# Two decode-attention problems in one kernel: batches of both taken in turn, weights in rings, loads in an order that a plan works out

## Chip, core and metric

The kernel runs on one core of one Trainium2 chip. The metric is device time in microseconds. Before the change the median of 6 runs is 285.73 us (282.39 to 287.11).

## What is computed

Two problems, A and B, each one token of grouped-query attention with 32 query heads on 16 key/value heads of 128, and a cache of 8,192 keys per head. A looks at the last 2,048 keys, B at all 8,192. All data are bfloat16. The result is the two output rows of 576, side by side.

```python
q = (x @ wq).reshape(B, Sq, Hq, Dh).transpose(0, 2, 1, 3)        # x: 1x1x576, wq: 576x4096
k = jnp.repeat(k_cache[:, :, Sk - W:, :], rep, axis=1)           # A: W = 2048; B: all 8192
v = jnp.repeat(v_cache[:, :, Sk - W:, :], rep, axis=1)           # rep = 2
scores = jnp.einsum("bhqd,bhkd->bhqk", q, k) * (Dh ** -0.5)
o = jnp.einsum("bhqk,bhkd->bhqd", softmax(scores), v)
out = o.transpose(0, 2, 1, 3).reshape(B, Sq, Hq * Dh) @ wo       # wo: 4096x576
```

Every byte is read once: per head 2.1 MB of keys and as much of values for B, 0.52 MB each for A, and per problem 4.7 MB of `wq` and of `wo`; in sum 102.8 MB.

## The kernel before

**Tiles and groups.** A key/value head of B has T = 64 tiles of 128 keys, one of A has 16. TensorE works in *groups* of eight tiles (GS = 8): 8 groups per head of B, 2 per head of A, 160 in all. For each group TensorE transposes eight key tiles into PSUM (`pe_tg`, L434), VectorE copies them to SBUF (`dve_copy`, L552), and TensorE multiplies them with the two query rows of the head (`pe_sg`, L458), one group behind.

**Batches.** Heads are put into batches; B has four of 4 heads, A has 4, 4, 4, 2 and 2 (`bsizes`). All of B comes first, then all of A. At the end of a batch its scores get a maximum (`dve_d1` L563, `pe_mxt` L470, `dve_d2d3` L572/L575, `pe_mxb` L477), ScalarE takes the exponentials (`act_batch` L599/L608), TensorE multiplies with the values (*PV*, `pe_pv` L487), sums the exponentials (`pe_z` L500), VectorE divides (`dve_norm` L584/L587), and TensorE multiplies with `wo` (`pe_outproj` L527), a 512-wide and a 64-wide matmul per query head. The whole problem is summed in one PSUM row (`bankP`), which ScalarE copies out at the end of each problem (`act_outcopy` L622/L625). The query projections (`pe_qproj_block` L410) are done in 16 blocks of four query heads.

**Order on TensorE.** It is fixed when the program is built. `hook` hangs a task behind the score step of a group, and never behind the last group, `NG - 1`. With L a batch's last group: `mxt` behind L+1, `mxb` behind L+3, the PVs of its heads behind L+6 and then every `dv` groups (8 for B, 2 for A), never before the PV of an earlier batch (`last_pv_pos`), the sum of exponentials with the last PV, the output projection four groups later. Tasks of one position keep the order in which they were hung. Query block number jg is hung behind group 5 jg - 1 or just before the first group of its heads, whichever is earlier.

**Loads.** All loads go through SyncE's queue, which issues in order and waits, where it must, for the buffer to be free; what is queued behind a waiting load waits too. Keys (L355) and values (L366) have three buffers each of one B head (2.1 MB), which also take four A heads each; `assign_regions` hands out places round and round, keys in the order of the heads, values in the order of the PVs. A key load waits for the last transposes, a value load for the PV, of the heads that had the place before. `wq` has two buffers (L320 and L325, a wait on the projection two blocks back), `wo` has a place for everything (L339). The loads are sorted by the place in TensorE's order at which they are needed:

```python
for h in heads:
    add_load(tindex[("tg", head_first_group[h["n"]])], (lambda h=h: dma_k(h, KQ)))
for h in heads:
    add_load(tindex[("pv", h["n"])] - 0.3, (lambda h=h: dma_v(h, KQ)))
loads.sort(key=lambda t: (t[0], t[1]))
for _, _, fn in loads:
    fn()
```

Of the kernel before, what the change touches and what calls it, by code (L numbers as in the profile page):

```python
# [125 lines left out]
def bass_concat_heads__sliding_block_cached__gqa_block_cached__decode_kernel(  # L126
# [14 lines left out]
    Dh = 128  # L141
# [15 lines left out]
    for pi, (x, kc, vc, wq, wo, nkeys, s0, ooff) in enumerate(  # L157
        [
            (B_x, B_k_cache, B_v_cache, B_wq, B_wo, Sk, 0, NOUT),
            (A_x, A_k_cache, A_v_cache, A_wq, A_wo, W, Sk - W, 0),  # L160
        ]
    ):
        T = nkeys // 128
        GS = min(8, T)
        assert T % GS == 0
        BH = min(Hkv, 512 // (rep * T), 4)
        G_ = T // GS
        bmin = max(1, -(-3 // G_))
        if pi == 1 and Hkv >= BH + 2 * max(2, bmin):
            tsz = max(2, bmin)  # L170
            bsizes = []
            left = Hkv - 2 * tsz
            while left > 0:
                bsizes.append(min(BH, left))
                left -= min(BH, left)
            bsizes += [tsz, tsz]
        else:
            bsizes = []
            left = Hkv
            while left > 0:  # L180
                bsizes.append(min(BH, left))
                left -= min(BH, left)
        assert sum(bsizes) == Hkv and all(0 < b <= BH for b in bsizes)
        probs.append(
            dict(pi=pi, x=x, k=kc, v=vc, wq=wq, wo=wo, T=T, s0=s0, GS=GS,
                 G=T // GS, BH=BH, bsizes=bsizes, NB=len(bsizes), ooff=ooff)
        )
# [5 lines left out]
    NS = 2  # L193

    with ExitStack() as es:
# [4 lines left out]
        wq_sb = [sb(f"wq_sb{i}", [128, NCH, HBQ * Dh], BF16) for i in range(2)]  # L200
        wo_sb = [sb(f"wo_sb{i}", [128, Hq, NOUT], BF16) for i in range(2)]
# [14 lines left out]
        outrow_sb = [sb(f"outrow{i}", [1, NOUT], BF16) for i in range(2)]  # L216

# [20 lines left out]
        for j in range(2):  # L238
            sems[f"wq{j}"] = sem(f"s_wqslot{j}")
        S = _Sched()  # L240

        heads = []
        for p in probs:
            bstart = []
            acc = 0
            for bsz in p["bsizes"]:
                bstart.append(acc)
                acc += bsz
            for g in range(Hkv):
                b = max(i for i in range(len(bstart)) if bstart[i] <= g)  # L250
                heads.append(dict(pi=p["pi"], g=g, T=p["T"], GS=p["GS"], G=p["G"],
                                  b=b, gl=g - bstart[b], qb=(g * rep) // HBQ))
# [15 lines left out]
        for p in probs:  # L268
            for b in range(p["NB"]):
                hs = [h for h in heads if h["pi"] == p["pi"] and h["b"] == b]  # L270
                batches.append(dict(pi=p["pi"], b=b, heads=hs,
                                    last_group=head_last_group[hs[-1]["n"]],
                                    first_group=head_first_group[hs[0]["n"]]))
# [32 lines left out]

        def wq_slot(pi, j):
            return (pi * NQB + j) % 2

        def dma_wq_block(p, j, q):  # L310
            pi = p["pi"]
            wq = p["wq"]
            c0, c1 = j * HBQ * Dh, (j + 1) * HBQ * Dh
            jg = pi * NQB + j
            slot = jg % 2
            waits = []
            if jg - 2 >= 0:
                pj = jg - 2
                waits.append(("pe", "qproj", pj // NQB, pj % NQB))
            S.add(q, lambda e: e.dma_start(wq_sb[slot][:, 0:nfull, :],  # L320
                                           wq[0:nfull * 128, c0:c1].rearrange("(c p) n -> p c n", p=128)),
                  waits=waits, inc=("wqdma", pi, j, 0), sem=f"wq{slot}")
            if D % 128:
                r = D % 128
                S.add(q, lambda e: e.dma_start(wq_sb[slot][0:r, nfull, :], wq[nfull * 128:D, c0:c1]),  # L325
                      inc=("wqdma", pi, j, 1), sem=f"wq{slot}")
# [3 lines left out]

        def dma_wo_batch(bt, q):
            pi = bt["pi"]
            p = probs[pi]
            hq0 = bt["heads"][0]["g"] * rep
            hq1 = (bt["heads"][-1]["g"] + 1) * rep
            semname = f"wo{bt['gb']}"
            if semname not in sems:
                sems[semname] = sem("s_" + semname)
            S.add(q, lambda e: e.dma_start(wo_sb[pi][:, hq0:hq1, :],  # L339
                                           p["wo"][hq0 * 128:hq1 * 128, :].rearrange("(h p) n -> p h n", p=128)),  # L340
                  inc=("wodma", bt["gb"]), sem=semname)
# [28 lines left out]

        def dma_out(p, q):
            pi, ooff = p["pi"], p["ooff"]
            S.add(q, lambda e: e.dma_start(out[0, 0:1, ooff:ooff + NOUT], outrow_sb[pi][0:1, :]),
                  waits=[("act", "oc2", pi)], inc=("outdma", pi), sem="out")
# [44 lines left out]
        def pe_tg(gi):  # L419
# [8 lines left out]
            if gi - NS >= 0:  # L428
                waits.append(("dve", "copy", gi - NS))
# [9 lines left out]
        def pe_sg(gi):  # L439
# [7 lines left out]
            waits = [("dve", "copy", gi)]  # L447
# [65 lines left out]
        def pe_outproj(bt):  # L513
            pi, gb = bt["pi"], bt["gb"]
            p = probs[pi]
            waits = [("dve", "oT", gb), ("wodma", gb)]
            if bt["b"] == 0 and pi == 1:
                waits.append(("act", "oc2", 0))
# [4 lines left out]
            lastbatch = (bt["b"] == p["NB"] - 1)  # L523
            for hq in range(hq0, hq1):
                for (c0, w) in out_chunks:
# [4 lines left out]
                        rhs=wo_sb[pi][:, hq, c0:c0 + w],  # L530
                        start=(hq == 0), stop=(hq == Hq - 1))),
                        waits=waits if k == 0 else [],
                        inc=(("pe", "outproj", pi) if lastbatch else ("pe", "outprojb", gb)) if last else None,
# [8 lines left out]

        def dve_copy(gi):
# [4 lines left out]
            bank = gi % NS  # L548
            waits = [("pe", "tg", gi)]
            if gi - NKT >= 0:  # L550
                waits.append(("pe", "sg", gi - NKT))
            S.add("dve", lambda e: e.tensor_copy(KTsb[kt][:, 0:GS, :], stage[bank][:, 0:GS * 128].rearrange(  # L552
                "p (g d) -> p g d", g=GS)),
                waits=waits, inc=("dve", "copy", gi), pb={"r": [f"S{bank}"]})
# [64 lines left out]
        def act_outcopy(p):  # L619
            pi = p["pi"]  # L620
            n1 = min(512, NOUT)
            S.add("act", lambda e: e.activation(outrow_sb[pi][0:1, 0:n1], bankP[0:1, 0:n1], ACT.Copy),  # L622
                  waits=[("pe", "outproj", pi)], inc=("act", "oc1", pi), pb={"r": ["P0"]})
            if NOUT > n1:
                S.add("act", lambda e: e.activation(outrow_sb[pi][0:1, n1:NOUT], bankP[0:1, n1:NOUT], ACT.Copy),  # L625
                      waits=[("act", "oc1", pi)], inc=("act", "oc2", pi), pb={"r": ["P1"]})
            else:
                S.add("act", lambda e: e.activation(outrow_sb[pi][0:1, 0:1], bankP[0:1, 0:1], ACT.Copy),
                      waits=[("act", "oc1", pi)], inc=("act", "oc2", pi), pb={"r": ["P0"]})
# [13 lines left out]
        for bt in batches:  # L643
            L = bt["last_group"]
            p = probs[bt["pi"]]
            dv = p["G"]
            pm = hook(L + 1, ("mxt", bt))
# [49 lines left out]

        TUNIT = min(p["T"] for p in probs)
# [36 lines left out]
        LEADW = 300  # L735
# [11 lines left out]
        wloads = []  # L747
        _lseq = [0]

        def add_load(pos, fn, lst=None):  # L750
            _lseq[0] += 1
            (loads if lst is None else lst).append((pos, _lseq[0], fn))

        for h in heads:
            add_load(tindex[("tg", head_first_group[h["n"]])], (lambda h=h: dma_k(h, KQ)))
        for p in probs:
            pi = p["pi"]
            add_load(min(tindex[("xt", pi)], tindex[("qproj", pi, 0)]) - 0.7, (lambda p=p: dma_x(p, WQ)),
                     wloads)
            for j in range(NQB):  # L760
                add_load(tindex[("qproj", pi, j)] - 0.5, (lambda p=p, j=j: dma_wq_block(p, j, WQ)), wloads)
        for h in heads:
            add_load(tindex[("pv", h["n"])] - 0.3, (lambda h=h: dma_v(h, KQ)))
        for bt in batches:
            add_load(tindex[("outprojb", bt["gb"])] - 0.2, (lambda bt=bt: dma_wo_batch(bt, KQ)))
        if WQ == KQ:
            loads = loads + wloads
            wloads = []
        loads.sort(key=lambda t: (t[0], t[1]))
        for _, _, fn in loads:  # L770
            fn()
        wloads.sort(key=lambda t: (t[0], t[1]))
        for _, _, fn in wloads:
            fn()
# [4 lines left out]
        cust = {"Q": [], "O": []}  # L779
        for kind, arg in pe_tasks:  # L780
# [37 lines left out]
            elif kind == "outprojb":  # L818
                bt = arg
                p = probs[bt["pi"]]  # L820
                pe_outproj(bt)
                if bt["b"] == p["NB"] - 1:
                    act_outcopy(p)
# [59 lines left out]
```

## Time and profile before

| | |
|---|---|
| device time, 6 runs | 285.22, 286.31, 285.30, 286.16, 282.39, 287.11 us; median 285.73 |
| the profiled execution | 284.68 us, of it 282.8 us span (first to last instruction) |
| busy share of the span | TensorE 84%, its weight loads 75%, VectorE 43%, ScalarE 8% |
| mean granted TensorE clock | 0.725 of full speed |
| DMA | 103.38 MB, mean 366 GB/s; SyncE's queue 94.5% and instruction fetch 0.8% of the 16 DMA engines' span |
| median from issue to landing | keys of B 14.7 us, values of B 15.8, `wo` of B 12.1, first part of `wq` of B 6.4 |

Columns of the groups below: line, engine, operation, output and input, count | busy us, mean ns of one | idle time of the engine before them and what ended most of it.

```profile
L552 DVE COPY ktsb<-stage 128x1024 bf16<-128x1024 bf16 x160 | 109.6, 691 | 103.9 <-PE stage L434 103.3
L434 PE MATMUL stage<-ident_b,kbuf 128*128 128x128 bf16 x1280 | 135.7, 270 | 18.9 <-issue 11.2
...
L458 PE MATMUL sc<-qT,ktsb 128*128 128x2 bf16 x1280 | 60.5, 168 | 11.0 <-issue 4.7
...
L487 PE MATMUL bankO<-pT,vbuf 128*128 128x2 bf16 x1280 | 36.8, 164 | 5.6 <-issue 3.7
```

TensorE carries the key transposes, the scores and the PVs; matmuls are pipelined, so the mean time of one is longer than its share of the busy time. "stage", "sc", "bankO", "bankP" and "bankQ" are PSUM tiles, "kbuf" and "vbuf" the buffers of keys and values. VectorE's idle time is mostly a wait for transposes. In the profile SyncE's queue is "SPq", and DMA share can pass 1 a little, because packets of one engine overlap.

### The profile page before, as it was taken

Reading aid. Unit: us, or ns where it says so; the run is one execution under the profiler, and the core shown is the slowest. Engines: PE = TensorE matmul, PEld = TensorE weight load, DVE = VectorE, ACT = ScalarE, POOL = GpSimd, SP = SyncE. Lnnn points to the kernel's source line nnn. Section 1 sums busy time; section 2 is a strip of 40 time slices with the busy share of each in tenths; the row PEclk is TensorE's granted clock in tenths of the full one; section 3 lists DMA queues with packets and bytes.
Section 4 is the critical chain, followed back from the end, with each engine's and each line's share of the span. In section 5 each row is a group of like instructions: output and inputs, shape, how many; then the busy total and the mean of one; then the engine's idle time right before and its main releaser. Section 6 shows DMA issues by size and latency. Waiting matters only on the chain.

```text
span 282.8 us, 9590 instructions
## 1 busy us (share of the span) xinstructions
PE 237.7 (84%) x4343; PEld 212.0 (75%) x4343; DVE 122.6 (43%) x225; ACT 23.1 (8%) x142; POOL 1.3 (0%) x9
## 2 busy tenths in 40 slices
PE   1699988999596999999968999589698899778775
PEld 1598887899596985998968798579577898774442
DVE  0257664545253551453534556346245466511010
ACT  1000000300000000300000030000002303302002
POOL 1000000000000000000000000000000000000000
PEclk9999995556657655955757588676877579955985
DMA  7989999999999999999999999999999975589990
GB/s 262 364 295 348 387 354 384 400 361 403 378 378 396 382 414 383 386 431 420 420 404 423 421 426 422 413 376 412 417 388 411 405 316 199 208 281 396 405 348 6
DMA packets 31935, 103.38 MB, mean 366 GB/s; under 512 B 2196, under 2 KB 19608, under 8 KB 27800
## 3 DMA queue, kind: packets, MB, share of 16 engines
q1 hardware_dynamic: 31896, 102.77, 94.5%
q8 instruction: 35, 0.57, 0.8%
q14 instruction: 4, 0.03, 0.0%
HBM read 102.76 MB, written 0.00 MB: 363 GB/s over the span
## 4 chain that ended last, share of the span: by engine, by line
PE 72%; DVE 10%; issue 9%; DMA 6%; ACT 1%; SPq 1%; DVEq 0%
PE stage L434 35%; PE bankO L487 11%; PE sc L458 10%; DVE ktsb L552 8%; PE bankQ L410 7%; PE bankP L527 6%; DMA wo_sb<-in_A_wo_dram 3%; DMA kbuf<-in_B_k_cache_dram 3%; PE bankQ L477 1%; PE bankO L500 1%; DVE mx L563 1%; SPq L366 1%; ACT pT L608 1%; PE bankQ L470 1%; DVE rz L584 0%
## 5 line engine op out<-in xcount | busy, mean ns | idle before, releaser
L552 DVE COPY ktsb<-stage 128x1024 bf16<-128x1024 bf16 x160 | 109.6, 691 | 103.9 <-PE stage L434 103.3
L434 PE MATMUL stage<-ident_b,kbuf 128*128 128x128 bf16 x1280 | 135.7, 270 | 18.9 <-issue 11.2
L434 PEld LDWEIGHTS stage<-ident_b,kbuf 128*128 128x128 bf16 x1280 | 102.7, 122 | 21.6 <-issue 13.1
L458 PE MATMUL sc<-qT,ktsb 128*128 128x2 bf16 x1280 | 60.5, 168 | 11.0 <-issue 4.7
L458 PEld LDWEIGHTS sc<-qT,ktsb 128*128 128x128 bf16 x1280 | 55.5, 106 | 16.6 <-DVE ktsb L552 9.4
L487 PE MATMUL bankO<-pT,vbuf 128*128 128x2 bf16 x1280 | 36.8, 164 | 5.6 <-issue 3.7
L487 PEld LDWEIGHTS bankO<-pT,vbuf 128*128 128x128 bf16 x1280 | 35.0, 99 | 6.8 <-issue 6.7
L527 PE MATMUL bankP<-wo_sb,oT 128*1 128x512 bf16 (+1 forms) x128 | 23.1, 346 | 3.9 <-DMA wo_sb<-in_A_wo_dram 2.4
L599 ACT ACTIVATE bias<-bankQ 128x8 f32<-128x8 f32 (+1 forms) x9 | 1.6, 177 | 250.4 <-PE bankQ L477 250.4
L410 PE MATMUL bankQ<-xT,wq_sb 128*128 128x1 bf16 (+1 forms) x320 | 20.2, 170 | 2.2 <-DVE xT L396 1.0
L410 PEld LDWEIGHTS bankQ<-xT,wq_sb 128*128 128x128 bf16 (+1 forms) x320 | 17.4, 100 | 4.5 <-DVE xT L396 1.2
L527 PEld LDWEIGHTS bankP<-wo_sb,oT 128*1 128x1 bf16 x128 | 8.6, 96 | 16.0 <-issue 10.4
L608 ACT ACTIVATE pT<-sc,bias 128x64 bf16<-128x64 f32 (+1 forms) x64 | 18.0, 316 | 0.3
L584 DVE RECIPROCAL rz<-bankO 128x8 f32<-128x8 f32 (+1 forms) x9 | 1.8, 202 | 30.8 <-PE bankO L500 30.8
L608 ACT ACTIVATION_READ_ACCUMULATOR pT<-sc,bias 128x1 f32 x64 | 13.7, 214 | 0.0
L540 DVE CAST qT<-bankQ 128x4 bf16<-128x4 f32 x16 | 2.6, 162 | 15.2 <-PE bankQ L410 15.2
L477 PE MATMUL bankQ<-diag,ones_f 8*128 8x8 f32 (+1 forms) x18 | 4.3, 308 | 0.6 <-DVE diag L575 0.6
L500 PE MATMUL bankO<-rsum,ones_f 128*128 128x8 f32 (+1 forms) x18 | 4.5, 325 | 0.0
L572 DVE TENSOR_REDUCE m<-bankQ 8x1 f32<-8x128 f32 (+1 forms) x9 | 2.4, 271 | 4.8 <-PE bankQ L470 4.8
L477 PEld LDWEIGHTS bankQ<-diag,ones_f 8*128 8x128 f32 (+1 forms) x18 | 3.5, 238 | 1.0 <-DVE diag L575 0.9
L563 DVE TENSOR_REDUCE mx<-sc 128x8 f32<-128x512 f32 (+2 forms) x9 | 4.0, 446 | 0.5 <-PE sc L458 0.5
L500 PEld LDWEIGHTS bankO<-rsum,ones_f 128*128 128x128 f32 x18 | 3.9, 270 | 0.0
(20 smaller groups left out, 13.8 us busy)
## 6 DMA issues: line engine op xcount, KB each, us to landing
vbuf<-in_B_v_cache_dram SPq DMA_DIRECT2D x16, 2048.0 KB, 15.8
kbuf<-in_B_k_cache_dram SPq DMA_DIRECT2D x16, 1792.0 KB, 14.7
kbuf<-in_A_k_cache_dram SPq DMA_DIRECT2D x32, 256.0 KB, 10.5
vbuf<-in_A_v_cache_dram SPq DMA_DIRECT2D x16, 512.0 KB, 7.9
wo_sb<-in_B_wo_dram SPq DMA_DIRECT2D x4, 1152.0 KB, 12.1
kbuf<-in_B_k_cache_dram SPq DMA_DIRECT2D x16, 256.0 KB, 10.7
wq_sb<-in_B_wq_dram SPq DMA_DIRECT2D x8, 512.0 KB, 6.4
wq_sb<-in_A_wq_dram SPq DMA_DIRECT2D x8, 512.0 KB, 8.5
```

The lines of the kernel that those rows point to most:

```text
L366: S.add(q, lambda e: e.dma_start(Vbuf[slot][:, row0:row0 + T, :], p["v"][0, g, s0:s0 + T * 128, :].rearrange("(p t) d -> p (t d)", p=128)) ...
L410: S.add("pe", (lambda e, hq=hq, c=c, rows=rows: e.matmul(bankQ[:, QT_COL[pi] + hq:QT_COL[pi] + hq + 1], lhsT=wq_sb[slot][0:rows, c, (hq - ...
L434: S.add("pe", (lambda e, i=i, t=t: e.transpose(stage[bank][:, i * 128:(i + 1) * 128], Kbuf[slot][:, krow + t, :], ident_b[:, :])), waits=w ...
L458: S.add("pe", (lambda e, i=i, col=col: e.matmul(sc[bank][:, col:col + rep], lhsT=KTsb[kt][:, i, :], rhs=qT_sb[pi][:, g * rep:(g + 1) * rep ...
L470: S.add("pe", lambda e: e.transpose(bankQ[0:nh, MXT_COL:MXT_COL + 128], mx_sb[pi][:, c0:c0 + nh], ident_f[:, :]), waits=[("dve", "d1", gb) ...
L477: S.add("pe", lambda e: e.matmul(bankQ[:, BIAS_COL:BIAS_COL + nh], lhsT=ones_f[0:nh, :], rhs=diag_sb[pi][0:nh, 0:nh], start=True, stop=Tru ...
L487: S.add("pe", (lambda e, t=t: e.matmul(bankO[:, col:col + rep], lhsT=Vbuf[slot][:, vrow + t, :], rhs=pT_sb[pi][:, g, t, :], start=(t == 0) ...
L500: S.add("pe", lambda e: e.matmul(bankO[:, Z_COL[pi] + c0:Z_COL[pi] + c0 + nh], lhsT=ones_f[:, :], rhs=rsum_sb[pi][:, c0:c0 + nh], start=Tr ...
L527: S.add("pe", (lambda e, hq=hq, c0=c0, w=w: e.matmul(bankP[0:1, c0:c0 + w], lhsT=oT_sb[pi][:, hq:hq + 1], rhs=wo_sb[pi][:, hq, c0:c0 + w], ...
L552: S.add("dve", lambda e: e.tensor_copy(KTsb[kt][:, 0:GS, :], stage[bank][:, 0:GS * 128].rearrange("p (g d) -> p g d", g=GS)), waits=waits, ...
L563: S.add("dve", lambda e: e.tensor_reduce(mx_sb[pi][:, c0:c0 + nh * rep], sc[bank][:, 0:nh * T * rep].rearrange("p (g t h) -> p g h t", g=n ...
L608: S.add("act", (lambda e, g=g, gl=gl, r=r, hq=hq, col0=col0: e.activation(pT_sb[pi][:, g, :, r], sc[bank][:, col0:col0 + T * rep].rearrang ...
```

## The change

- **Order of batches.** Batches of B and A are taken in turn, in proportion to their number. A's batches become 4, 4, 4, 3 and 1 heads.
- **Rings.** `wq` gets eight buffers for two. `wo` gets four buffers of one batch each, in place of one place for all heads; a load waits for the projection four batches back.
- **Accumulation.** Each batch's output projection is a sum of its own in `bankP`, and VectorE adds it to a row in SBUF (`dve_outacc`); ScalarE's copies at the end of a problem are gone. An output projection waits for the sum of the one before it.
- **Spacing.** The last batch of a problem, other than the very last batch, gets another `dv` for its PVs.
- **Order of loads.** Each load has a place where its buffer becomes free (`ready`), one where it is needed (`need`), and its bytes. When the program is built, a loop steps through TensorE's order with assumed durations and an assumed bandwidth, and issues, as long as fewer than 5 MB are on their way, the load with the earliest need among the ready ones. Only the order that comes out of it is used.
- `COPY_ACT_EVERY`, by which ScalarE could take a part of the key copies, is 0.

```diff
-        if pi == 1 and Hkv >= BH + 2 * max(2, bmin):
-            tsz = max(2, bmin)
+        if pi == 1 and Hkv >= BH + bmin + 2:
...
+            if bmin > 1:
+                tail = [bmin + 1, 1]
...
-            bsizes += [tsz, tsz]
+            bsizes += tail
...
+    NWQ = 8
+    NWO = 4
+    COPY_ACT_EVERY = 0
...
-        wq_sb = [sb(f"wq_sb{i}", [128, NCH, HBQ * Dh], BF16) for i in range(2)]
-        wo_sb = [sb(f"wo_sb{i}", [128, Hq, NOUT], BF16) for i in range(2)]
+        wq_sb = [sb(f"wq_sb{i}", [128, NCH, HBQ * Dh], BF16) for i in range(NWQ)]
+        BQMAX = max(max(p["bsizes"]) for p in probs) * rep
+        wo_sb = [sb(f"wo_sb{i}", [128, BQMAX, NOUT], BF16) for i in range(NWO)]
...
+        while ia < len(la) or ib < len(lb):
+            if ia < len(la) and (ib >= len(lb) or ia * len(lb) <= ib * len(la)):
+                order.append(la[ia])
+                ia += 1
+            else:
+                order.append(lb[ib])
+                ib += 1
         heads = []
...
+        for hs in order:
+            heads.extend(hs)
...
+            waits = []
+            if gb - NWO >= 0:
+                waits.append(ev_outproj_done(batches[gb - NWO]))
+            S.add(q, lambda e: e.dma_start(wo_sb[slot][:, 0:hq1 - hq0, :],
                                            p["wo"][hq0 * 128:hq1 * 128, :].rearrange("(h p) n -> p h n", p=128)),
...
-        def pe_outproj(bt):
+        def pe_outproj(bt, xw=()):
...
-            waits = [("dve", "oT", gb), ("wodma", gb)]
-            if bt["b"] == 0 and pi == 1:
-                waits.append(("act", "oc2", 0))
+            waits = [("dve", "oT", gb), ("wodma", gb)] + list(xw)
...
-                        rhs=wo_sb[pi][:, hq, c0:c0 + w],
-                        start=(hq == 0), stop=(hq == Hq - 1))),
+                        rhs=wo_sb[gb % NWO][:, hq - hq0, c0:c0 + w],
+                        start=(hq == hq0), stop=(hq == hq1 - 1))),
...
-        def act_outcopy(p):
...
+        def dve_outacc(bt):
...
+            if b == 0:
+                dst = outrow_sb[pi] if lastb else oacc_sb[pi][0]
+                S.add("dve", lambda e: e.tensor_copy(dst[0:1, :], bankP[0:1, 0:NOUT]),
+                      waits=[("pe", "outprojb", gb)], inc=("dve", "oacc", gb), pb={"r": banks})
             else:
+                src = oacc_sb[pi][(b - 1) % 2]
+                dst = outrow_sb[pi] if lastb else oacc_sb[pi][b % 2]
+                S.add("dve", lambda e: e.tensor_tensor(dst[0:1, :], bankP[0:1, 0:NOUT], src[0:1, :], ALU.add),
+                      waits=[("pe", "outprojb", gb), ("dve", "oacc", gb - 1)], inc=("dve", "oacc", gb),
+                      pb={"r": banks})
...
+            if bt["gb"] < len(batches) - 1 and bt["b"] == p["NB"] - 1:
+                dv = max(3, -(-p["T"] * 35 // (p["GS"] * 92)))
...
         for h in heads:
-            add_load(tindex[("tg", head_first_group[h["n"]])], (lambda h=h: dma_k(h, KQ)))
+            ready = max([tindex[("tg", head_last_group[m])] for m in h["kprev"]], default=-1)
+            T = h["T"]
+            add_load(ready, tindex[("tg", head_first_group[h["n"]])], (lambda h=h: dma_k(h, KQ)),
+                     T * 128 * 128 * 2, 2 if T > h["GS"] else 1, ("k", h["n"]))
...
+            ready = max([tindex[("pv", m)] for m in h["vprev"]], default=-1)
+            add_load(ready, tindex[("pv", h["n"])], (lambda h=h: dma_v(h, KQ)),
+                     h["T"] * 128 * 128 * 2, 1, ("v", h["n"]))
...
+        BW = 370e3
+        ISSUE_NS = 0.65
+        INFLIGHT = 5.0e6
...
+        for i in range(len(pe_tasks)):
+            kind, arg = pe_tasks[i]
+            while True:
+                now = t_pe
+                inflight_bytes[:] = [(tc, b) for (tc, b) in inflight_bytes if tc > now]
+                if sum(b for _, b in inflight_bytes) >= INFLIGHT:
+                    break
+                cands = [by_seq[q] for q in pending_set if by_seq[q]["ready"] < i]
+                if not cands:
+                    break
+                ld = min(cands, key=lambda d: (d["need"], d["seq"]))
+                issue(ld, now)
+            for ld in loads_of_task.get(i, []):
+                if ld["seq"] in pending_set:
+                    assert ld["ready"] < i
+                    issue(ld, t_pe)
...
+            t_end[i] = start + task_dur(kind, arg)
+            t_pe = t_end[i]
...
+        for ld in loads_in_order:
+            ld["fn"]()
...
-                pe_outproj(bt)
-                if bt["b"] == p["NB"] - 1:
-                    act_outcopy(p)
+                pe_outproj(bt, xw=cust["P"])
+                dve_outacc(bt)
+                cust["P"] = [("dve", "oacc", bt["gb"])]
```

## The prediction

> **What bounds the kernel now.** I read the table of stretches first, because shares over the whole span mix stages. Columns: us, busy time of each engine, granted TensorE clock, DMA share, GB/s.
>
> ```profile
> 14.00:28.00 14.00, 13.67 (x249) 12.81 (x247) 8.86 (x16) 0.00 (x0) 0.00 (x0) 1.00 0.89 319
> 28.00:42.00 14.00, 12.88 (x265) 11.51 (x262) 9.09 (x16) 0.00 (x0) 0.00 (x0) 0.99 1.04 368
> 42.00:224.00 182.00, 158.78 (x2905) 146.12 (x2901) 84.24 (x145) 11.50 (x75) 0.00 (x0) 0.65 1.03 402
> 224.00:252.00 28.00, 24.60 (x596) 23.30 (x593) 15.30 (x32) 6.14 (x46) 0.00 (x0) 0.80 0.69 256
> 252.00:273.00 21.00, 16.88 (x232) 10.51 (x230) 2.01 (x8) 2.11 (x11) 0.00 (x0) 0.80 1.05 394
> 273.00:282.80 9.80, 5.35 (x53) 2.96 (x51) 0.84 (x4) 2.11 (x11) 0.00 (x0) 0.55 0.21 76
> ```
>
> From 42 to 224 us the DMA never rests (1.03) while TensorE idles 23 of 182 us: problem B is bound by transfers. DMA rests only in four places. With 1.03 as full, they are worth 1.9 us in the first 7 us (share 0.75 there), 14 x (1 - 0.89/1.03) = 1.9 at 14 to 28, 28 x (1 - 0.69/1.03) = 9.2 at 224 to 252, and 9.8 x (1 - 0.21/1.03) = 7.8 at the end. Their sum is 20.8, so the queue share, 95.3% of 282.8 us, is 262 us of full DMA. I use this as a clock: x MB of the 102.8 have landed at 1.9 + 2.55x us at the earliest.
>
> Next SyncE's waits (us in total, times, longest), and its issues around the largest hole (start, us, line, transfer, count).
>
> ```profile
> SPq L320 <- PE bankQ L410: 68.1, 14, 8.9
> ...
> SPq L366 <- PE bankO L487: 25.7, 3, 9.9
> ```
> ```profile
> 216.65 1.40 SPq L366 DMA_DIRECT2D vbuf<-in_B_v_cache_dram  x1
> 227.98 19.63 SPq L366 DMA_DIRECT2D vbuf<-in_A_v_cache_dram  x9
> 247.65 0.82 SPq L339 DMA_DIRECT2D wo_sb<-in_B_wo_dram  x1
> ```
>
> The 68.1 us are waits for a free wq buffer of two; only the 1.9 us at 14 to 28 can come from them, since DMA was full otherwise. At 217 all keys of A are already issued, and SyncE stands before A's values until B's last heads have done their PV: values lag keys, and the three value buffers hold 2.1 MB each of B. That is the hole. Then the prices: from the timeline, one group of eight tiles at half clock, the first 2.1 MB load and a B head's PV; from the chain of waits (start, us, what), the pieces of its end.
>
> ```profile
> 134.37 1.01 PE L434 MATMUL stage<-ident_b,kbuf 128*128 128x128 bf16 x8
> ...
> 135.43 1.01 PE L434 MATMUL stage<-ident_b,kbuf 128*128 128x128 bf16 x8
> ```
> ```profile
> 0.74 0.88 SPq L355 DMA_DIRECT2D kbuf<-in_B_k_cache_dram  x2
> ...
> 8.63 1.04 PE L434 MATMUL stage<-ident_b,kbuf 128*128 128x128 bf16 x8 [3.34 <-DMA kbuf<-in_B_k_cache_dram]
> ...
> 139.15 1.75 PE L487 MATMUL bankO<-pT,vbuf 128*128 128x2 bf16 x64
> ```
> ```profile
> 256.62 3.86 PE bankP L527 x16
> ...
> 272.76 1.14 PE bankP L527 x8
> ...
> 276.35 1.08 PE bankO L487 x32
> ...
> 278.33 2.09 PE bankP L527 x8
> ```
>
> So a group costs 1.07 us at half clock (start to start) and 0.80 at full (four key copies start between 24.62 and 27.83), a PV 1.75, an output projection of 8 query heads (16 matmuls) 3.9 at half clock and, by the last batch's 8 matmuls in 1.14, some 2.3 at full; a 2.1 MB load on an empty queue lands in under 7.9 us.
>
> TensorE's clock: the rows at 134 to 136 run back to back and still at the half rate; the granted clock averages 0.65 over 182 us in which TensorE was 87% busy. [...]
>
> **The change, part by part.** *Order.* Batches now run B0 A0 A1 B1 A2 B2 A3 B3 A4 (from the test `ia * len(lb) <= ib * len(la)` with 4 and 5 batches). Counts of groups, heads and batches stay 160, 32 and 9; A's last batches become 3 and 1 heads for 2 and 2. Bytes are the same, so the 262 us of DMA stay. What moves is the hole: after the last key there were A's small values, now there are B3's four, 8.4 MB, and only three fit at a time.
>
> *Rings.* Eight wq buffers for two remove most L320 waits: worth at most 1.9 us of DMA. Four wo slots add waits on L339 for the projection four batches back; the loads behind it on SyncE would wait too. The slot of B2's weights is free after A0's projection, some 90 groups earlier, so I take 0; were it not, the price is one median wo landing, 12.1 us.
>
> *Issue order.* Loads go out by need among those whose buffer is free, at most 5 MB ahead in the plan. SyncE waits only on its buffers, not on the plan's clock, so it can at best keep DMA full, which it was in B. Nothing for 42 to 224 us.
>
> *Accumulation.* Nine VectorE sums of 1x576 from PSUM replace four ScalarE copies (0.59 and 0.21 us each pair). No such row: 0.39 us by the copy's rate (691 ns for 1024 columns), 0.77 by the reduce's (680 ns for 512); I take 0.7, nearer in type to the reduce. Key copies queue behind each, covered by 104 us of VectorE waiting for TensorE; uncovered, 9 x 0.7 = 6.3 us. TensorE now waits for a sum where two projections stand together (before A0, A1, A2, A3): 4 x 0.9 with the semaphores. One is in the end's sum below; the rest lie under DMA.
>
> *Spacing.* The new `dv` is for B3 alone, whose PV positions are already past the last group and are cut to it: nothing. `COPY_ACT_EVERY` is 0: nothing.
>
> *PV clumps.* Positions never decrease, so A0's, A1's, A2's and A3's PVs all land with the fourth PV of the B batch before (group L+30). Each stands behind a norm, 0.9 us (277.43 to 278.33, end of PV to projection). Under DMA in the middle, counted at the end.
>
> *The end, summed.* Call B2's last group 0; the last group is 40. B3's fourth key load needs group 14 done and is used at 31. After it in order of need come V of B3's first head 2.1, A4's keys 0.5, V of heads 2 and 3 4.2, wo 1.5, V of the fourth head 2.1, A4's V 0.5: 10.9 MB. So it lands at 1.9 + 2.55 x 91.9 = 236; if B2's and A3's wo (2.1 MB, needed at 34) are behind it, 231; if the last wo (1.5 MB) is ahead, 240. I take 234. Then: transposes 1.1, scores 0.4, PV 1.75, norm 0.9, A3's PVs 1.3, sums of exp 0.7, ten groups 9.6 (between 0.8 and 1.07 each), B2's projection 3.3, the sum 0.9, A3's projection 2.5: 22.4, so keys end at 256.4. V of heads 2 and 3 wait for the PVs at 30 (some 238) and have landed by 257. Then bias and first exp 1.5, PV 1.75, and only now may V of the fourth head be issued (third buffer of three): 7.2 us (between 2.1 MB at 413 GB/s, 5.1, and 7.9; nearer the measured load). PV 1.75, norm 0.9, projection 3.4, then A4's whole chain: maximum and bias 1.5, exp 1.0, PV 0.55, norm 0.9, projection 1.05, sum 0.85, store 1.7: 7.5. That is 24.0 and a span of 280.4. The profiled execution took 284.68 with a span of 282.8, 1.9 outside: 282.3 us against 284.68 profiled and a median of 285.73. In short: the hole of 9.2 us closes, and about two thirds of it return as the wait for the fourth V and a longer last chain.
>
> **The rivals.** *DMA's floor.* The fourth key load is early (231) and groups run at 0.8 us; then V of the fourth head stands right behind the third in a full queue, and DMA ends at 1.9 + 262 = 264. After it 13.5 us remain of the chain: 277.5, with 1.9 some 279. For it: the 5 MB cap keeps the queue fed. Against: granted clock 0.65. If bytes moved at the 413 GB/s of 119 to 217 us throughout, 249 us of DMA would do, and the end would be TensorE's; I let the range reach 275.
>
> *Slower: prefetch ahead of keys.* Transfers of one queue land in order, and a key load released at group 14 stands behind whatever wo, wq and V has been issued meanwhile. If the last wo and B3's first V (3.6 MB, 9 us) go ahead, the fourth key load lands at 243, and all after it is one chain: 234 becomes 243, 291 us. It decides from a landing after 240. For it: SyncE's loads land a median 14.7 us after issue already. Against: order by need puts keys first.
>
> *It does nothing.* The rings and order only move waits that DMA hid: a span near 282, 284 to 286.
>
> [...]
>
> **How the numbers follow.** A run here tells 1% (282.9 to 288.6) from no change. Forecast 0.38, own range 279 to 286, split evenly at 282.9; DMA's floor 0.25, all faster; slower rival 0.32, all beyond 288.6; nothing 0.05, all within. So faster 0.44, within 0.24, slower 0.32. The range 275 to 292 takes in the floor and the slower rival's middle and leaves out some 0.2, most of it above.
>
> **What would show it.** DMA share stays near 1.03 from 14 us to about 255, and no hole at 224 to 252. Keys end at 254 to 259. SyncE's last L366 waits for a PV; TensorE then idles 3 to 5 us before B3's fourth PV, and 13 to 15 us pass from that landing to the end. TensorE held at keys before group 31 past 240 shows the slower rival. Holes in the middle, or a rate away from 400 GB/s, would make all of it wrong.

## The result, and the profile after

| | time, us | span of the profiled execution | granted clock in it | ratio to the kernel before, 95% interval |
|---|---|---|---|---|
| before | median 285.26 (10 runs) | 282.8 | 0.725 | |
| after | median 290.27 (288.26 to 295.43, 5 runs) | 284.9 (286.63 us with what lies around it) | 0.774 | 1.016 (1.010 to 1.022) |
| after, again, on another occasion | median 288.94 (12 runs) beside 286.14 before | 286.7 | 0.757 | 1.010 (1.006 to 1.014) |

Ratios, here and below, are formed from the runs within 1.5% of the fastest of their kernel. The change makes the kernel 1.0 to 1.6% slower. 282.3 us and a gain were forecast; the time lies inside the range of 275 to 292, on the wrong side. First the table of stretches of the kernel after (us, busy time of each engine, granted clock, DMA share, GB/s).

```profile
42.00:100.00 58.00, 51.83 (x1021) 49.02 (x1020) 28.59 (x57) 7.33 (x51) 0.00 (x0) 0.69 1.04 397
100.00:224.00 124.00, 102.50 (x1900) 89.54 (x1901) 59.10 (x103) 9.47 (x64) 0.00 (x0) 0.78 1.01 395
```
```profile
245.00:252.00 7.00, 6.04 (x80) 4.60 (x78) 3.84 (x7) 0.00 (x0) 0.00 (x0) 0.78 1.02 431
252.00:260.00 8.00, 6.30 (x103) 4.60 (x103) 5.07 (x10) 0.59 (x4) 0.00 (x0) 1.00 0.69 264
260.00:273.00 13.00, 7.06 (x257) 7.01 (x258) 0.00 (x0) 2.07 (x14) 0.00 (x0) 0.56 0.60 227
273.00:284.90 11.90, 6.65 (x43) 2.94 (x43) 2.61 (x8) 0.79 (x5) 0.00 (x0) 0.64 0.00 0
```

DMA is full until 252 us, as forecast: the hole at 224 to 252 us is gone. It comes back behind the last key, as a thin stretch (0.69, 0.60) and an empty one. TensorE's waits in the kernel after (us in total, times, longest):

```profile
PE sc L495 <- issue: 10.8, 7, 3.0
PE bankO L524 <- issue: 10.5, 8, 2.7
PE stage L471 <- DMA kbuf<-in_B_k_cache_dram: 7.8, 2, 4.3
PE bankO L524 <- DMA vbuf<-in_B_v_cache_dram: 5.6, 1, 5.6
...
PE bankO L524 <- DVE oT L631: 2.4, 4, 0.6
PE bankP L560 <- DVE oacc_0 L670: 1.7, 2, 0.8
```

The same view of the kernel before had these rows:

```profile
PE stage L434 <- issue: 11.2, 5, 3.1
PE stage L434 <- DMA kbuf<-in_B_k_cache_dram: 7.6, 2, 4.3
```

Keys make TensorE wait twice in either kernel, both times in the first 9 us, and never after. That row of the kernel before was there to be read before the prediction, and contradicts it: with DMA at 1.03 for 182 us, TensorE still waited for no key. So was the profile's line on the chain of work that ended last, as shares of the span, which names TensorE and hardly DMA:

```profile
PE 72%; DVE 10%; issue 9%; DMA 6%; ACT 1%; SPq 1%; DVEq 0%
```

The new wait is the one for values, 5.6 us; its place shows in SyncE's issues and in the chain that ended last (start, us, what):

```profile
234.77 10.13 SPq L401 DMA_DIRECT2D vbuf<-in_B_v_cache_dram  x3
...
262.18 0.33 SPq L401 DMA_DIRECT2D vbuf<-in_B_v_cache_dram  x1
```
```profile
260.39 1.78 PE bankO L524 x64
262.18 8.89 DMA vbuf<-in_B_v_cache_dram
271.12 1.87 PE bankO L524 x64
...
273.92 4.01 PE bankP L560 x16
```

The first PV of B's last batch frees its buffer at 262.18, the load for the fourth head goes out at that moment and lands 8.9 us later.

### The profile page after: what moved, and what is told of

Same layout as the page of the kernel before. It is cut to its first block, busy times and chain, and to the rows that moved or that the text cites. A ratio compares the mean times of both kernels' runs of the same rounds, so it can differ in the third digit from the quotient of the medians.

```text
span 284.9 us, 9626 instructions
## 1 busy us (share of the span) xinstructions
PE 228.4 (80%) x4343; PEld 201.2 (71%) x4343; DVE 128.2 (45%) x234; ACT 21.5 (8%) x138; POOL 1.3 (0%) x9
## 4 chain that ended last, share of the span: by engine, by line
PE 68%; DVE 14%; issue 11%; DMA 6%; SPq 0%; ACT 0%; DVEq 0%
PE stage L471 30%; PE bankO L524 11%; PE sc L495 11%; DVE ktsb L594 9%; PE bankP L560 7%; PE bankQ L447 6%; DMA vbuf<-in_B_v_cache_dram 3%; DMA kbuf<-in_B_k_cache_dram 3%; PE bankO L537 1%; PE bankQ L514 1%; DVE oacc_1 L675 1%; DVE mx L607 1%; DVE oacc_0 L670 1%; DVE oacc_0 L675 1%; DVE outrow L675 1%
## 5 line engine op out<-in xcount | busy, mean ns | idle before, releaser
L471 PE MATMUL stage<-ident_b,kbuf 128*128 128x128 bf16 x1280 | 125.4, 256 | 11.6 <-DMA kbuf<-in_B_k_cache_dram 7.8
L471 PEld LDWEIGHTS stage<-ident_b,kbuf 128*128 128x128 bf16 x1280 | 94.9, 115 | 14.3 <-DMA kbuf<-in_B_k_cache_dram 8.1
L495 PEld LDWEIGHTS sc<-qT,ktsb 128*128 128x128 bf16 x1280 | 52.8, 103 | 25.1 <-DVE ktsb L594 12.3
L524 PEld LDWEIGHTS bankO<-pT,vbuf 128*128 128x128 bf16 x1280 | 35.3, 101 | 19.3 <-issue 13.7
L560 PE MATMUL bankP<-wo_sb,oT 128*1 128x512 bf16 (+1 forms) x128 | 20.5, 320 | 4.3 <-DVE oacc_0 L670 1.7
L628 DVE RECIPROCAL rz<-bankO 128x8 f32<-128x8 f32 (+2 forms) x9 | 1.8, 202 | 37.0 <-PE bankO L537 37.0
L652 ACT ACTIVATION_READ_ACCUMULATOR pT<-sc,bias 128x1 f32 x64 | 13.6, 213 | 0.0
L607 DVE TENSOR_REDUCE mx<-sc 128x8 f32<-128x512 f32 (+3 forms) x9 | 4.0, 448 | 2.5 <-PE sc L495 2.5
L537 PE MATMUL bankO<-rsum,ones_f 128*128 128x8 f32 (+2 forms) x18 | 5.0, 349 | 0.0
L514 PE MATMUL bankQ<-diag,ones_f 8*128 8x8 f32 (+2 forms) x18 | 4.1, 295 | 1.1 <-DVE diag L619 1.0
L675 DVE TENSOR_TENSOR oacc_1<-bankP,oacc_0 1x576 f32<-1x576 f32 x3 | 2.2, 745 | 5.5 <-PE bankP L560 5.5
L514 PEld LDWEIGHTS bankQ<-diag,ones_f 8*128 8x128 f32 (+2 forms) x18 | 3.2, 223 | 1.7 <-DVE diag L619 1.4
```

The lines of the kernel that those rows point to most:

```text
L471: S.add("pe", (lambda e, i=i, t=t: e.transpose(stage[bank][:, i * 128:(i + 1) * 128], Kbuf[slot][:, krow + t, :], ident_b[:, :])), waits=w ...
L495: S.add("pe", (lambda e, i=i, col=col: e.matmul(sc[bank][:, col:col + rep], lhsT=KTsb[kt][:, i, :], rhs=qT_sb[pi][:, g * rep:(g + 1) * rep ...
L514: S.add("pe", lambda e: e.matmul(bankQ[:, BIAS_COL:BIAS_COL + nh], lhsT=ones_f[0:nh, :], rhs=diag_sb[pi][0:nh, 0:nh], start=True, stop=Tru ...
L524: S.add("pe", (lambda e, t=t: e.matmul(bankO[:, col:col + rep], lhsT=Vbuf[slot][:, vrow + t, :], rhs=pT_sb[pi][:, g, t, :], start=(t == 0) ...
L537: S.add("pe", lambda e: e.matmul(bankO[:, Z_COL[pi] + c0:Z_COL[pi] + c0 + nh], lhsT=ones_f[:, :], rhs=rsum_sb[pi][:, c0:c0 + nh], start=Tr ...
L560: S.add("pe", (lambda e, hq=hq, c0=c0, w=w: e.matmul(bankP[0:1, c0:c0 + w], lhsT=oT_sb[pi][:, hq:hq + 1], rhs=wo_sb[gb % NWO][:, hq - hq0, ...
```

## Experiments

The theories. **Transfers** (the prediction): DMA bounds the kernel, so bytes and DMA holes are time. **TensorE**: its instructions and waits pace the run, DMA merely keeps up. Ratios are to the kernel before, run beside each.

**e1 and e16: half of the PV matmuls, in both orders.**

```diff
-            for t in range(T):
+            for t in range(T // 2):
...
-                    start=(t == 0), stop=(t == T - 1))),
+                    start=(t == 0), stop=(t == T // 2 - 1))),
```

> The kernel before with half of the PV matmuls left out (640 for 1280; the output is then that of half the values); every byte is still loaded. TensorE loses 640 x 29 ns = 18 us of work. If the kernel is bound by transfers, as the prediction said of 42 to 224 us, the time stays at 282 to 286 us, since the 262 us of full DMA, the start and the end are as before. If TensorE paces it and DMA merely keeps up, 265 to 272 us.

> The changed kernel with half of the PV matmuls left out (the output is then that of half the values), all bytes loaded: 18 us less of TensorE's work, as in e1. If TensorE paces the new order too, 272 to 281 us, with waits for keys in the middle as in e1; if DMA bounds it, 287 to 291.

Before: 276.71 us, 0.9685 (0.963 to 0.974), 9 us less. After: 278.51 us, 0.9737 (0.969 to 0.978), some 11 less than the changed kernel. Less TensorE work is less time in both orders, by about half to two thirds of the 18 us. Where the rest went, TensorE's waits and the chain that ended last show, in e1 and then in e16:

```profile
PE stage L434 <- DMA kbuf<-in_B_k_cache_dram: 19.1, 11, 4.6
PE bankO L487 <- DMA vbuf<-in_A_v_cache_dram: 5.6, 8, 0.9
```
```profile
DMA 54%; PE 33%; DVE 5%; issue 3%; SPq 2%; ACT 1%; DVEq 0%
```
```profile
PE stage L471 <- DMA kbuf<-in_B_k_cache_dram: 10.6, 3, 5.2
PE bankO L524 <- DMA vbuf<-in_B_v_cache_dram: 7.1, 1, 7.1
```
```profile
PE 75%; DMA 12%; DVE 6%; issue 5%; SPq 2%; DVEq 0%
```

In e1 nine more waits are for keys, and DMA leads the chain. So TensorE paces both kernels, and in the old order DMA is the next bound, about 9 us below. In e16 only one wait for keys is new (2.1 us), and TensorE still leads, in an execution with a low clock (0.592); that DMA is the next bound of the new order too, some 11 us below, is likely but not shown. The time of e16 lies near the 279 us that the prediction called DMA's floor, but not by its sum: the last load lands at 267.2 us and not at 264, and the fourth V still waits for a PV.

**e2: half of the value bytes.**

```diff
-                Vbuf[slot][:, row0:row0 + T, :],
-                p["v"][0, g, s0:s0 + T * 128, :].rearrange("(p t) d -> p (t d)", p=128)),
+                Vbuf[slot][:, row0:row0 + T // 2, :],
+                p["v"][0, g, s0:s0 + T * 64, :].rearrange("(p t) d -> p (t d)", p=128)),
...
-                    lhsT=Vbuf[slot][:, vrow + t, :],
+                    lhsT=Vbuf[slot][:, vrow + t // 2, :],
```

> The kernel before with half of each value load left out (each loaded tile is used twice, so half of the values are not read); TensorE's work is as before, the bytes fall from 102.8 to 81.8 MB. Bound by transfers: 21 MB x 2.55 us = 53 us of DMA go and TensorE becomes the bound, 255 to 265 us. Paced by TensorE: 278 to 286 us, if the stretches that the profile calls issue (some 18 us on the chain before) stay; if these come from instruction blocks that are fetched behind data in full DMA engines, they shrink and the time is 266 to 276 us with granted clocks unchanged.

280.54 us, 0.979 (0.974 to 0.984). A fifth of all bytes is worth 5 us; transfers as the bound asked for 20 to 30. TensorE's wait for A's `wo`, 2.4 us in the kernel before, is gone in e2; what the rest of the 5 us is was not traced. The guess about the stretches called "issue" fell too: they are 22.9 us here, with emptier DMA engines (share 0.88 from 42 to 224 us), where the kernel before has 20.0.

**e3: the DMA hole closed in the old order.**

```diff
             dv = p["G"]
+            if bt["gb"] < len(batches) - 1 and bt["b"] == p["NB"] - 1:
+                dv = max(3, -(-p["T"] * 35 // (p["GS"] * 92)))
```

> The kernel before with the change's new spacing alone: B's last four PVs stand 4 groups apart in place of 8, so value buffers come free earlier in the first groups of A and the DMA hole at 224 to 252 us shrinks. If a DMA hole costs time, 277 to 281 us. If TensorE paces that stretch (it was busy 24.6 of 28 us there), 283 to 287 us, no change.

0.9995 (0.995 to 1.004): no change. The stretch in e3:

```profile
224.00:252.00 28.00, 24.02 (x416) 21.11 (x417) 9.49 (x19) 5.31 (x36) 0.00 (x0) 0.52 1.03 381
```

DMA share there rose from 0.69 to 1.03, and TensorE was as busy as before (24.0 for 24.6 us). The granted clock in the stretch was 0.52 in this execution, for 0.80 before, so the two stretches are not alike; that nothing was gained is said by the ratio. The 9.2 us of DMA rest that the prediction counted as the gain were worth nothing.

**e4 and e8: a fourth value buffer, and its control.**

```diff
-    NSV = 3
+    NSV = 4
...
-    NWQ = 8
+    NWQ = 4
```

> The changed kernel with four value buffers and, to make room, four wq buffers. The last B head's values no longer wait for a PV after the last key. If the wait before that PV (5.6 us in the profile after) is what the new order costs at the end, 283 to 286 us where the changed kernel has 290. If the loss is spread over the whole run, 288 to 291 us.

> The changed kernel with four wq buffers for eight, the control for the run with four value buffers (286.8 us): 288 to 291 us, as with eight, if the wq ring is hidden and the value buffer alone made the difference; 285 to 287 if the smaller ring did.

With four value buffers 1.0004 (0.997 to 1.004); the control, with the second edit alone, 290.48 us and 1.021 (1.012 to 1.031). The wait for values is gone from e4's profile, and the loss with it. So the loss is shown by taking its cause away; wq's four further buffers are worth nothing.

**e6 and e7: the order undone, the plan undone.**

```diff
-            if ia < len(la) and (ib >= len(lb) or ia * len(lb) <= ib * len(la)):
+            if ia < len(la):
```
```diff
-        loads_in_order = [by_seq[q] for q in issue_order]
+        loads_in_order = sorted(loads, key=lambda d: (d["need"], d["seq"]))
```

> The changed kernel with the old order of batches (all of B, then all of A); rings, load plan, sums on VectorE and A's batches of 4, 4, 4, 3, 1 stay. If the interleaving alone is what costs, 283 to 286 us, as before. If rings, plan or sums cost, 288 to 291 us.

> The changed kernel with its loads sorted by the place at which they are needed, without the plan. TensorE is held by a load only at the start and before the fourth PV of B's last batch, so the plan should be worth nothing: 288 to 292 us. If the plan keeps keys from being late, they are late here: waits of the transposes for keys in the middle, above 293. If the plan's order costs, 285 to 287.

All of B first, with everything else of the change: 286.11 us, 1.003 (0.998 to 1.008), as before. Sorted loads in the new order: 291.46 us, 1.023 (1.014 to 1.032), as after. The interleaving, on three value buffers, is what costs; in the old order rings, plan and sums on VectorE together cost nothing that can be measured, and in the new one the plan brings nothing.

**e5 and e9: B's last batch ahead of A's last two, and then wo planned early.**

```diff
-            if ia < len(la) and (ib >= len(lb) or ia * len(lb) <= ib * len(la)):
+            if ia < len(la) and (ib >= 3 or ia * len(lb) <= ib * len(la)):
```
```diff
-            add_load(ready, tindex[("outprojb", gb)], (lambda bt=bt: dma_wo_batch(bt, KQ)),
+            add_load(ready, max(ready + 1, tindex[("tg", bt["first_group"])]), (lambda bt=bt: dma_wo_batch(bt, KQ)),
```

> The changed kernel with the order B0 A0 A1 B1 A2 B2 B3 A3 A4: B's last batch ends before A's last two, so its four PVs run among A's last eight groups (and the new spacing of 4 takes effect). If the wait for the fourth value load behind the last key is what the change costs (5.6 us in the profile after, and a last chain that begins with four B heads), 281 to 285 us. If the loss comes from waits for sums and norms or from the load order, which stay, 288 to 291 us.

> The kernel of e5 (B's last batch before A's last two) with each wo load planned as if needed at its batch's first group, so that it no longer stands behind value loads that wait for a PV. In e5 the last wo of B was issued at 263.2 us and TensorE idled for it and for the fourth value load. If that wait was what ate the gain, some 5 us less than e5, 286 to 289 us; if the serial chains of three batches behind the last key are (norm, projection, maximum, exponentials one after another), it stays at 290 to 294.

Both missed: 1.017 (1.001 to 1.033) and 1.049 (1.041 to 1.057). In e5 eight groups of A are too few for four PVs spaced 4 apart from the sixth group on: three still pile up behind the last key, with two chains of A behind them, and four value loads, which wait for PVs, take SyncE 27 us, with the last wo behind them:

```profile
235.87 27.27 SPq L401 DMA_DIRECT2D vbuf<-in_B_v_cache_dram  x4
263.18 0.43 SPq L374 DMA_DIRECT2D wo_sb<-in_B_wo_dram  x1
```

In e9 the wo loads went ahead of keys and values needed sooner: three more waits for keys, and a first wait for x, together 5.1 of the 6.9 us between the medians of e5 and e9.

**e10 to e13 and e17: shorter ends.** In all of them A's batches are 4, 4, 4, 2, 2 heads again. e10 moves A's last batch ahead of B's last. e11 gives B batches of 4, 4, 4, 2, 2, puts its last two heads at the end and plans wo early as e9 does; e12 adds a fourth value buffer. e13 is e11 without the early wo, e17 is e13 with four value buffers. The order of e11, e12, e13 and e17:

```diff
+        order = [la[0], lb[0], lb[1], la[1], lb[2], la[2], la[3], lb[3], lb[4], la[4]]
         heads = []
```

> The changed kernel with A's last batch moved ahead of B's last one (and A's batches 4, 4, 4, 2, 2, since a batch of 2 groups can't stand there): the kernel ends with B's four heads and no chain of A's behind them. In the profile after, A4's chain runs alone from 277.9 us to the end; its maximum, exponentials, PV and norm leave the end, some 5 us. Paced by TensorE's chain: 284 to 287 us, with the wait for the fourth value load still there. If only bytes or granted clock count: 289 to 292.

> Order B0 A0 A1 B1 A2 B2 B3 A3 A4 B4 with B's batches 4, 4, 4, 2, 2 and A's 4, 4, 4, 2, 2, wo loads planned early. Behind the last key stand only two PVs of B, one norm, one projection of 8 matmuls and the store, some 10 us where the changed kernel has 26; two PVs and one projection move ahead of it (5 us of work), and the wait for a value buffer goes. If the end's chain is what separates these kernels: 277 to 281 us, below both. If DMA bounds it: not below 279 (262 us of full DMA, 2 at the start, the chain behind the last bytes).

> As the one before, with four value buffers and four wq buffers. If no value load waits at the end any more with three, no difference, 277 to 281 us; if one still does, 1 to 4 us less than with three.

> As e11 (B's batches 4, 4, 4, 2, 2 with its last two heads at the very end), but with each wo load planned by its projection again, so that no wo stands ahead of the first keys. In e11 TensorE waited 13.1 us for keys, most of it early. If those waits cost e11 its 294 us, 283 to 287 us; and if TensorE's own work paces the run, it can't fall much below the kernel before (285.9), since moving work ahead of the last key doesn't remove it. If the serial chain behind the last key is time that nothing else fills, 277 to 281 us.

> As e13, with four value buffers and four wq buffers. In e13 TensorE still stands for A's values near the end (SyncE behind a PV, then 8.2 us to landing). If that wait is real time, 2 to 4 us less than e13's 283 to 288, thus 280 to 285 and below the kernel before; if TensorE's clock gives back what a wait costs, no difference.

e10: 1.012 (1.002 to 1.021), no better than after: its last key's scores end some 6 us later, because what left the end now stands ahead of it. e11 and e12: 1.034 (1.027 to 1.040) and 1.037 (1.032 to 1.043): what the prediction's slower rival feared, loads ahead of keys, in another kernel and earlier in it (three further waits for keys, between 82 and 120 us). TensorE's waits in e11:

```profile
PE stage L468 <- DMA kbuf<-in_B_k_cache_dram: 13.1, 5, 4.3
```

e13, wo back in its place: 287.88 us, some 6 us less than e11. Its times fall into two clusters, 282.9 to 286.5 and, twice as many, 287.7 to 289.8; the ratio of 0.993 (0.988 to 0.998) is formed from the first, and the median of all is above the 286.22 of the kernel before, so it is no gain to rely on. e17: 1.011 (1.006 to 1.017), not below e13, so the forecast of e17 failed. Nothing here beats the kernel before. Why e17 is not at e13's time is open.

**e14, e15 and e18.** e14 splits the first head's keys (8, 8, 16, 32 tiles) in the kernel before; e15 sorts A's wo to its batch's first group as well. e18 is the changed kernel again; its result stands in the first table.

```diff
+            if n == 0:
+                parts = [(0, GS), (GS, 2 * GS), (2 * GS, 4 * GS), (4 * GS, T)]
```
```diff
-            add_load(tindex[("outprojb", bt["gb"])] - 0.2, (lambda bt=bt: dma_wo_batch(bt, KQ)))
+            add_load(tindex[("outprojb", bt["gb"])] - 0.2 if bt["pi"] == 0 else tindex[("tg", bt["first_group"])], (lambda bt=bt: dma_wo_batch(bt, KQ)))
```

> The kernel before with the first head's keys in four loads (8, 8, 16, 32 tiles), the last two behind x and the first wq block, so that TensorE's second group need not wait for 2.1 MB; nothing else is changed. In the profile before TensorE idles from 5.3 to 8.6 us for it. If TensorE paces the run, about 3 us carry to the end: 281.5 to 284 us. If DMA bounds it (its bytes and its start are as before), 285 to 287 us.

> As e14, and A's wo loads sorted to the first group of their batch, ahead of the values that wait for PVs. In the profile before TensorE waits 2.4 us for A's wo on the last chain, and SyncE stands 9.9 us there. If waits on TensorE's chain add up, 2 us less than e14, 279 to 282 us; if wo is hidden or its bytes delay A's keys, 282 to 285.

> The changed kernel itself once more, with more rounds: 288 to 292 us and a ratio of 1.01 to 1.02 to the kernel before, if the first five runs were typical; e17 is read against it on one chip.

e14: 1.003 (0.998 to 1.008); e15: 1.004 (1.000 to 1.007); neither gained. In e14's profile the first query projection starts at 8.99 us in place of 10.62, just behind its `wq`, which landed at 8.90 (the profile calls that wait "issue"): 1.6 us were gained and not 3. Later stands a wait that the kernel before does not have, for keys of the second head; here e14 and then the same group of tiles in the kernel before:

```profile
8.99 1.30 PE L414 MATMUL bankQ<-xT,wq_sb 128*128 128x1 bf16 x20 [2.66 <-issue]
...
20.90 1.03 PE L441 MATMUL stage<-ident_b,kbuf 128*128 128x128 bf16 x8 [1.59 <-DMA kbuf<-in_B_k_cache_dram]
```
```profile
21.13 0.68 PE L434 MATMUL stage<-ident_b,kbuf 128*128 128x128 bf16 x8
```

These keys landed at 20.85 us, where they were there at 17.36 before, and of the gain 0.2 us is left. From 21 to 28 us the granted clock is at 0.50, where the kernel before had 1.00; whether the early start brought it down, or only this one execution had it, was not tried.

## Why the prediction was wrong

**The step that failed** is the first one: "From 42 to 224 us the DMA never rests (1.03) while TensorE idles 23 of 182 us: problem B is bound by transfers." Full DMA and a partly idle TensorE were read as cause and effect without asking what the idle time waited for. Of the 23 us 18.6 are "issue", none is for keys. e1, e2 and e16 show TensorE as the pace, with DMA some 9 us below in the old order; e3 shows that closing the DMA hole gains nothing. With that, "the hole of 9.2 us closes" stopped being a gain, and the new wait at the end, 5.6 us, had nothing to pay for it.

**The sum of the end** hung on the landing of B3's fourth key load at 234 us. That load landed at 225.1, earlier than any place that the prediction gave it (231 to 243). TensorE reached that head's first group at 238.4 on its own, without a wait:

```profile
238.41 0.61 PE L471 MATMUL stage<-ident_b,kbuf 128*128 128x128 bf16 x8
```

That is 4.4 us behind the 234. From there to the end of the scores it took 20.5 us for the 22.4 forecast; the value load 8.9 for 7.2; from its landing to the end 13.8 for 13.55. Together 4.5 us: a span of 284.9 for 280.4. So the mechanism at the end, four heads on three buffers and one load behind a PV, was right, and its price near; the pace up to it was taken from the wrong engine. That keys end so near the forecast is luck: the load came 9 us earlier than reckoned, and what TensorE needs to get there was not reckoned at all. Against a typical run the sum falls some 2 to 4 us shorter still: the profiled execution had the shortest time of its set, and the highest clock (0.774; the others 0.717 to 0.763).

**Costs called hidden.** The waits for sums and norms were put under DMA. TensorE paces the middle, so they count: waits other than for DMA and issue are 11.8 and 13.6 us in the two profiles of the kernel after, 9.1 before, 13.7 in e4. But e4 carries them too and is no slower than the kernel before, so they do not show as a separate loss.

**Right:** the rings and the new spacing bring nothing (e6 for all of it together, e8 for wq; B3's PVs are held back by the last group, as forecast), the plan nothing (e7), DMA full to about 252. **The slower rival** as priced, prefetch ahead of keys, did not happen in the changed kernel (225.1 us, where it decides after 240); e9 and e11 show what early wo loads cost. The loss came from the term that the forecast itself carried. Its sentence "Transfers of one queue land in order" is nearly so: in the kernel before 5 of 137 loads land ahead of the one issued just before them, by up to 1.4 us.

## What to carry to other kernels

A full queue isn't yet a bound: look at what the busiest compute engine waits for, and if no row names a transfer, a hole in DMA may be closed without gain (e3: share 0.69 to 1.03, ratio 0.9995). When two bounds lie as near to each other as here (285 and 277 us in the old order), halving one side's work and then the other's tells more than any reordering. In a reordered pipeline, ask what is left behind the last load of the leading stream, and whether the buffers of the lagging one can hold it: four heads on three buffers cost a PV of 1.78 us and a load of 8.9 us in series here, with TensorE waiting 5.6 us.

## What the hardware showed

**TensorE stops at fixed places of its instruction stream.** The stretches called "issue" stand in the middle of a run of matmuls, where no semaphore is waited for. The kernel after:

```profile
154.47 0.17 PE L495 MATMUL sc<-qT,ktsb 128*128 128x2 bf16 x1
...
157.69 0.34 PE L495 MATMUL sc<-qT,ktsb 128*128 128x2 bf16 x7 [3.05 <-issue]
```

The places are fixed in the stream. Counted in TensorE's instructions (matmuls, weight loads and waits in order of start), such stops stand at the 5059th, 5314th, 5827th, 6083rd and 6594th in the kernel after, and at the same numbers in e18, another execution of the same kernel. The steps are 255, 513, 256 and 511: one or two times 256. The profile has a queue for instructions, 35 packets in all, so 16 KB each:

```profile
q8 instruction: 35, 0.57, 0.8%
```

Each of the seven longest stops between 90 and 240 us overlaps one of these packets in time (155.3 to 156.4 in the stop from 154.6 to 157.7). That the stops are waits for instructions is read from these two coincidences; no run changes how instructions are fetched. All stretches called "issue" are 20 us before and 25 after, up to 3.1 us each; a few are something else (the 1.05 us before the PV at 260.39 end when ScalarE has its exponentials). They stay with a fifth of the bytes gone (e2, 22.9 us) and shrink to 7.6 and 10.1 us where TensorE has less to do (e1, e16). What sets the length of a stop was not tried.

**The clock can stay at half while TensorE is busy without a gap.** In the kernel after, from 60 to 80 us (TensorE busy 20.00 of 20 us, granted clock 0.50):

```profile
60.00:80.00 20.00, 20.00 (x376) 19.57 (x373) 10.02 (x21) 2.33 (x17) 0.00 (x0) 0.50 1.03 420
```

In e16, one run had a mean clock of 0.592 and took 280.56 us, the three others 0.742 to 0.774 and 278.35 to 278.58: there, a fifth of the clock went with 2 us.

**The granted clock of the first microseconds does not fit the matmuls.** It stands at 1.00 from 14 to 21 us of the kernel before, where the transposes of a group take 1.01 us and start 1.07 us apart, as at 134 us with a clock of 0.50.
